# A gated recurrence with a highway layer on one core: wider GpSimd products, e written over d in three pieces, zero matmuls in the ramp, and a new instruction list

## The chip, the cores and the metric

The kernel runs on 1 core of one Trainium2 chip. The metric is the device time of one execution in microseconds (us). Three runs of the kernel before gave 211.63, 212.32 and 211.7 us, a median of 211.7 us. The profile is one further execution, taken by the hardware profiler.

## What is computed

```python
sig = 1 / (1 + exp(-f_logit));  f = lower_bound + (1 - lower_bound) * sig;  i = 1 - f
for t in range(S):                       # x, f_logit: (4, 6336, 256) float32
    h = f[:, t] * h + i[:, t] * x[:, t];  y[:, t] = h
H = maximum(y @ w_h, 0);  T = 1 / (1 + exp(-(y @ w_t + b_t)))    # 25344 tokens, 256 x 256 weights
out = T * H + (1 - T) * y
```

## The kernel before, in words

The 25,344 tokens are cut into 28 units of 2, 2, 4, then 23 times 8, then 4 and 2 blocks of 128 tokens. A unit's data lie once with the tokens and once with the 256 features on the partitions; the features are two halves h = 0, 1 of 128. The work is a hand-ordered list of tokens (the string `order`); a token such as `z16.1:2` names a step, a unit, a half or piece, and, behind the colon, the buffer that its result takes. Every engine gets its instructions in the order of the list. The engines are PE (TensorE), DVE (VectorE), ACT (ScalarE), POOL (GpSimd) and SP, which issues all loads and stores. The steps of a unit are:

- `l`, `x` (line 262): loads of f_logit and x by SP, six buffers each. `w` (L393): a store of up to four blocks by SP, after the copy `c`.
- `u` (L274, ACT): sigmoid(-f_logit), all blocks in one instruction. Three buffers.
- `b` (L282): bv = u * x in pieces of 512 columns (two blocks), on POOL, or on DVE where the token ends in v.
- `i` (L288, PE): transposes of u into PSUM; `f` (L299 ACT, L297 DVE with v): f = 1 - (1 - lower_bound) u from there; `p` (L308, PE): transposes of bv. One-bank PSUM tiles `a`, two of them, hold both.
- `s` (L325, DVE): the scan y over a unit's tokens, one instruction for each half (and one more where a sequence starts). It begins from the last column of the unit before, so the scans of a half hang on each other.
- `z`, `g` (L337 and L140, PE): y @ w_t and y @ (w_h - 1), in two-bank PSUM tiles `b`, three of them, shared with `o`.
- `t` (L350, ACT): sigmoid(z + b_t). `d` (L354, DVE): max(g, -y) in the scaling of y used inside; three buffers.
- e = d * t (L359) in a tile of its own with three buffers: `E` are pieces of 512 columns on POOL up to a column that is set for each unit (the last number in `units`), `e` is the rest in one instruction on DVE. A unit of 8 blocks has 2,048 columns.
- `o` (L378, L379, PE): y and e are transposed back and added in PSUM, four blocks at a time; `c` (L388 ACT, L386 DVE with v) copies this to SBUF.

Once at the start: eight matmuls of zeros (L178), `pc` transposes the parameters, `cc`, `dg`, `WT`, `WH` (L223 to L251, DVE) scale weights and diagonals, `wh`, `wt` load weights (L215, L212), and `k*16` puts sixteen matmuls of zeros on PE. Where a POOL product follows a DVE product in the list, the helper `shared` lets POOL's instruction wait until the DVE one has ended. There is no wait the other way.

Of the kernel before, what the change touches and what calls it, by code (L numbers as in the profile page):

```python
# [19 lines left out]
def kernel(  # L20
# [54 lines left out]
z0.1:1 l4:4 i2.0:1 x4:4 b2.0:2 p1.1:0 b2.1 f2.0:0 z0.0:2 d0.0 s1.1 i2.1:1 t0.1:0 g1.1:0 b3.2v:0 p2.1:0 z1.0:1 t0.0  # L75
f2.1:1 b3.1v s2.1:2 t1.0:1 z1.1:2 p2.0:1 l5:5 t1.1 s2.0 b3.3 g1.0:1 u4:2 d1.1:1 b3.0 l6:0 i3.0:0 p3.1:1 E0.0:0 d1.0
s3.1:3 z2.1:0 z2.0:1 g2.1:2 f3.0:3 b4.2:1 i4.0:0 t2.0:2 g2.0:1 t2.1 d2.0:2 E1.0:1 b4.1 f4.0:1 x5:5 b4.0 l7:1 p3.0:1
x6:0 b4.3 u5:0 i4.1:0 s3.0 o1.0:1 f4.1:0 o0.0:0 d2.1 E2.0:2 p4.0:1 c0.0v:0 c1.0:1 s4.0:1 i5.0:0 g3.1:2 u6:1 d3.1:0
z3.0:1 E2.1 b5.3:2 f5.0:2 t3.0:0 i5.1:1 p4.1:0 g3.0:2 b5.1 o2.0:0 b5.0 z3.1:1 s4.1 f5.1:3 b5.2 d3.0 w0.0 p5.0:1 w1.0
b6.2:0 u7:2 b6.3 i7.1:0 z4.1:2 s5.0:0 t3.1 g4.0:1 l8:2 f7.1:1 p5.1:0 i6.1:1 c2.0:2 x7:1 z4.0:0 x8:2 t4.1:1 d4.0:1  # L80
f6.1:0 b6.1 g4.1:2 s5.1 z5.1:1 b6.0 w2.0 u8:0 t4.0 E3.0:1 l9:3 t5.1:2 e3 b7.3:1 d4.1 p6.1:0 i8.1:1 o3.0:0 o3.1:2
s6.1:2 b7.1 f8.1:2 E4.0:0 c3.0:3 i6.0:1 e4 f6.0:3 b8.1:2 l10:4 g5.0:1 p6.0:0 i7.0:1 c3.1:0 g5.1:0 o4.0:2 d5.0:2 z5.0:1
# [5 lines left out]
b11.1:2 s9.0 l14:2 t8.1 f10.1:0 o6.0:0 d8.1 i11.1:1 c6.0:1 b10.1 e8:0 e7:2 g9.0:1 z9.0:2 p10.0:0 f11.1:1 b11.2 o6.1:0
p10.1:1 t9.0:0 o7.0:2 b11.0 b12.2:0 b11.3 d9.0:0 z9.1:1 u13:2 b12.3 c6.1:2 b12.1 s10.0:2 i11.0:0 g9.1:0 s10.1 w6.0
t9.1 o7.1:1 p11.0:1 l15:3 c7.0:0 f11.0:3 c7.1:3 u14:0 E9.1:1 d9.1 E9.0 x13:1 i12.0:0 z10.0:2 w7.0 g10.0:1 o8.1:0  # L90
s11.0:3 d10.0:1 p11.1:1 t10.0:1 z10.1:1 g10.1:2 s11.1 b12.0 w6.1 c8.1:1 f12.0:0 w7.1 t10.1 g11.0:0 E9.2 o8.0:1 u15:1
E9.3 d10.1 p12.1:0 c8.0:0 x14:2 d11.0:2 w8.1 i13.1:1 s12.1:1 x15:3 b13.3:1 o9.1:2 b13.0 w8.0 z11.0:1 b13.1 f13.1:3
b13.2 c9.1:2 i15.1:1 p12.0:0 g11.1:0 e10:2 f15.1:1 i13.0:1 w9.1 z11.1:2 t11.0:2 s12.0 o9.0:1 p13.0:0 b14.2:2 f13.0:2
# [148 lines left out]
    def do_k(slot):  # L242
        busy(once["idle"])
# [120 lines left out]
    def do_e(n, k, eng, slot):  # L364
        times(n, nc.vector, units[n][6], NH * tokens(n), slot)
# [68 lines left out]
```

## Time and profile before

| what | us |
|---|---|
| median of the three runs | 211.7 |
| span of the profiled execution | 210.1 |
| DVE busy in the span | 193.0 |
| ACT busy in the span | 194.5 |
| PE busy in the span | 192.2 |
| POOL busy in the span | 174.0 |

The profiled execution's own time beside its span isn't given; the median of the runs is 1.6 us above the span. Busy times are unions: an instruction begins before the one ahead of it on its engine has drained, so the durations of a group add up to a little more than its engine's busy time. In a group's row stand the line, the engine, the operation, the shapes, the count, the busy time, the mean duration in ns, and behind the second bar the engine's idle time just before, with what ended it. In a row of the timeline stand the start, the duration, the engine and the instruction.

### The profile page before, as it was taken

The numbers are of one execution on the slowest core, as the hardware profiler recorded it, in microseconds if no ns is written. First come the engines' busy times: TensorE is split into PE (matmuls) and PEld (weight loads), VectorE is DVE, ScalarE is ACT, GpSimd is POOL, SyncE is SP. The second block draws the span as 40 slices with busy tenths as digits, with TensorE's granted clock in tenths as the row PEclk, the third lists the DMA queues.
The fourth block names the chain that finished last, engine by engine and source line by source line (L and its number), as shares of the span: only waits on it lengthen the run. The fifth ranks groups of instructions, "written<-read, shape, count | busy, mean of one in ns | idle before, by whom it ended". The sixth has DMA issues, their size and how long they took to land.

```text
span 210.1 us, 4667 instructions
## 1 busy us (share of the span) xinstructions
PE 192.2 (91%) x1819; PEld 132.4 (63%) x1819; DVE 193.0 (92%) x154; ACT 194.5 (93%) x190; POOL 174.0 (83%) x166
## 2 busy tenths in 40 slices
PE   7967798899989989999999999999999899999981
PEld 2444555576655766767576667657775676776760
DVE  0689999999999999999999999999999999999950
ACT  4678999999999999999999999999999999997882
POOL 3068989789999599978999999889879969999630
PEclk9999999999999999999999999999999999999998
DMA  6999999999999999999999999999999998463486
GB/s 223 392 426 421 410 418 424 420 415 420 410 428 413 420 420 403 331 406 387 387 427 416 409 416 423 418 417 396 333 428 416 416 413 332 188 271 132 172 328 254
DMA packets 15982, 78.69 MB, mean 374 GB/s; under 512 B 1748, under 2 KB 2264, under 8 KB 10072
## 3 DMA queue, kind: packets, MB, share of 16 engines
q1 hardware_dynamic: 15952, 78.39, 92.9%
q8 instruction: 14, 0.23, 0.5%
q14 instruction: 8, 0.07, 0.1%
q10 hardware_dynamic: 8, 0.00, 0.0%
HBM read 52.43 MB, written 25.95 MB: 373 GB/s over the span
## 4 chain that ended last, share of the span: by engine, by line
DVE 34%; PE 34%; DMA 12%; issue 8%; POOL 5%; ACT 3%; SPq 1%; POOLq 0%; DVEq 0%; ACTq 0%
DVE y L325 21%; DMA x<-in_x_dram 12%; DVE d L354 10%; PE op L379 5%; PE op L378 5%; PE g L337 4%; PE z L337 4%; PE bT L308 4%; POOL bv L282 4%; PE g L140 4%; PE uT L288 4%; PE z L140 3%; DVE e L359 3%; ACT t L350 2%; ACT o L388 1%
## 5 line engine op out<-in xcount | busy, mean ns | idle before, releaser
L282 POOL TENSOR_TENSOR bv<-u,x 128x512 bf16<-128x512 f16 x96 | 110.2, 1178 | 22.3 <-DVE w_sb L235 8.9
L325 DVE TENSOR_TENSOR_SCAN y<-f,y,bT 128x1024 bf16<-128x1024 f16 (+5 forms) x54 | 107.2, 1994 | 1.4 <-issue 0.4
L359 POOL TENSOR_TENSOR e<-d,t 128x512 bf16<-128x512 bf16 (+1 forms) x59 | 65.0, 1125 | 8.3 <-DVE e L359 5.0
L354 DVE SCALAR_TENSOR_TENSOR d<-y,ncc,g 128x1024 bf16<-128x1024 bf16 (+2 forms) x56 | 63.1, 1140 | 1.8 <-PE g L337 1.3
L350 ACT ACTIVATE t<-z,bt 128x1024 bf16<-128x1024 f32 (+2 forms) x56 | 58.4, 1066 | 2.7 <-PE z L140 1.5
L299 ACT ACTIVATE f<-uT,ncc 128x1024 f16<-128x1024 f16 (+2 forms) x54 | 57.8, 1079 | 2.0 <-ACT f L299 1.0
L388 ACT COPY o<-op 128x1024 f32<-128x1024 f32 (+1 forms) x50 | 52.3, 1058 | 1.9 <-PE op L379 1.0
L274 ACT ACTIVATE u<-l 128x2048 f16<-128x2048 f32 (+2 forms) x28 | 49.0, 1760 | 4.1 <-DMA l<-in_f_logit_dram 4.1
L378 PE MATMUL op<-diag,y 128*128 128x128 f16 x396 | 49.4, 219 | 0.8 <-ACT t L350 0.5
L379 PE MATMUL op<-ident_b,e 128*128 128x128 bf16 x396 | 49.4, 219 | 0.6 <-POOL e L359 0.6
L379 PEld LDWEIGHTS <-e 128*128 128x128 bf16 x396 | 44.0, 113 | 4.6 <-POOL e L359 1.1
L378 PEld LDWEIGHTS <-y 128*128 128x128 bf16 x396 | 44.2, 113 | 2.5
L337 PE MATMUL z<-y,w_sb 128*128 128x512 bf16 (+1 forms) x112 | 39.2, 367 | 2.0 <-DVE d L354 1.0
L337 PE MATMUL g<-y,w_sb 128*128 128x512 bf16 (+1 forms) x112 | 39.6, 367 | 0.5 <-DVE y L325 0.3
L308 PE MATMUL bT<-ident_f,bv 128*128 128x128 f32 x198 | 31.9, 278 | 4.1 <-DVE y L325 1.9
L288 PE MATMUL uT<-ident_h,u 128*128 128x128 f16 x396 | 31.1, 220 | 4.5 <-DVE y L325 3.3
L288 PEld LDWEIGHTS <-u 128*128 128x128 f16 x396 | 26.3, 98 | 13.9 <-issue 7.4
L140 PE MATMUL g<-y,w_sb 128*128 128x512 bf16 x92 | 34.9, 379 | 0.0
L140 PE MATMUL z<-y,w_sb 128*128 128x512 bf16 x92 | 34.8, 379 | 0.0
L337 PEld LDWEIGHTS <-w_sb 128*128 128x128 f16 x224 | 21.6, 98 | 16.2 <-issue 0.8
L308 PEld LDWEIGHTS bT<-ident_f,bv 128*128 128x128 f32 x198 | 22.3, 141 | 12.0 <-POOL bv L282 4.5
L140 PEld LDWEIGHTS <-w_sb 128*128 128x128 f16 x184 | 17.9, 98 | 18.2 <-issue 3.9
(35 smaller groups left out, 47.1 us busy)
## 6 DMA issues: line engine op xcount, KB each, us to landing
out_dram<-o SPq DMA_DIRECT2D x48, 512.0 KB, 6.1
l<-in_f_logit_dram SPq DMA_DIRECT2D x23, 1024.0 KB, 10.2
x<-in_x_dram SPq DMA_DIRECT2D x23, 1024.0 KB, 11.1
l<-in_f_logit_dram SPq DMA_DIRECT2D x2, 512.0 KB, 9.2
x<-in_x_dram SPq DMA_DIRECT2D x2, 512.0 KB, 6.0
l<-in_f_logit_dram SPq DMA_DIRECT2D x3, 256.0 KB, 6.1
x<-in_x_dram SPq DMA_DIRECT2D x3, 256.0 KB, 5.4
out_dram<-o SPq DMA_DIRECT2D x3, 256.0 KB, 5.4
```

Source lines behind the costliest of these rows:

```text
L140: return pe.add_instruction(mybir.InstMatmult(name=nc.get_next_instruction_name(), start_tensor_calc=start, stop_tensor_calc=stop, tile_si ...
L282: shared(pin(e.tensor_mul(st[n]["bv"][:, k].rearrange("p d j -> p j d"), st[n]["u"][:, q:q + 2], st[n]["x"][:, q:q + 2])), not eng)
L288: pin(nc.tensor.transpose(uT[:, j * P:(j + 1) * P], st[n]["u"][:, j, h * P:(h + 1) * P], ident_h))
L299: pin(nc.scalar.activation(to, of, AF.Identity, scale=ncc[:, h:h + 1], bias=1.0))
L308: pin(nc.tensor.transpose(words[:, k:k + g * (P - 1) + 1:g], pair, ident_f))
L325: pin(nc.vector.tensor_tensor_scan(y[:, c:e], st[n]["f", h][:, c:e], st[n]["bT", h][:, c:e], 0.0 if fresh else carry[h], op0=ALU.mult, op1 ...
L337: pin(nc.tensor.matmul(p[:, a:e], w, half(n, "y", ki)[:, a:e], start=ki == 0, stop=ki == NH - 1))
L350: pin(nc.scalar.activation(half(n, "t", m), st[n]["z", m][:, :tokens(n)], AF.Sigmoid, bias=bt[:, m:m + 1]))
L354: pin(nc.vector.scalar_tensor_tensor(half(n, "d", m), half(n, "y", m), ncc[:, m:m + 1], st[n]["g", m][:, :tokens(n)], op0=ALU.mult, op1=AL ...
L359: shared(pin(eng.tensor_mul(st[n]["e"][:, a:e], st[n]["d"][:, a:e], st[n]["t"][:, a:e])), eng is nc.gpsimd)
L378: pin(nc.tensor.matmul(o, half(n, "y", h)[:, cols], diag[:, h], start=True, stop=False))
L379: pin(nc.tensor.matmul(o, half(n, "e", h)[:, cols], ident_b, start=False, stop=True))
```

## The change

- `b` is cut by a table: one piece of 512 columns for units of 2 blocks, two of 512 for 4 blocks, two of 1,024 for 8 blocks. POOL has 45 pieces of 1,024 and 5 of 512 for 96 of 512; DVE has two of 512 and one of 1,024 for three of 512.
- `E` and the tile e are gone. `e` is d = d * t, in place, in pieces: 256 + 256 columns (2 blocks), 512 + 512 (4 blocks), 1,024 + 512 + 512 (8 blocks). A token with v runs on DVE, one without on POOL. DVE has 11 pieces of 1,024, 12 of 512 and 3 of 256; POOL has 12 of 1,024, 38 of 512 and 3 of 256. `o` reads d. d has four buffers, and u has four.
- `k` takes a PSUM tile of the given buffer in place of a fixed one, and eight `k*4` (four matmuls of zeros each) and one matmul of zeros ahead of z3.1 stand in the list's first part.
- The list is a new one on all engines. DVE has five f for two (0.0, 0.1, 1.1 and 27.0 with 256 columns, 8.0 with 1,024), and the one copy on DVE is c25.1 (1,024 columns) in place of c0.0 (512). l27 is loaded ahead of l13.

```diff
+    parts = [2] * 2 + [4] + [8] * 23 + [4] + [2]
+    for nb in parts:
+        units.append((nb, at, {2: (0, 1), 4: (0, 1, 2), 8: (0, 2, 4)}[nb], {2: (0, 256, 512), 4: (0, 512, 1024), 8: (0, 1024, 1536, 2048)}[nb]))
     order = """
-pc:1 l0:0 u0:0 l3:1 wh cc dg i0.0:1 x0:0 i0.1:0 k*16 u3:1 wt WH b0.0v:0 l1:2 f0.0:0 f0.1:1 p0.1:0 i3.1:1 u1:2 s0.1:0
-WT p0.0:0 x1:1 s0.0 f3.1:2 l2:3 x2:2 i1.1:0 u2:0 g0.1:2 f1.1:3 i1.0:1 d0.1:0 g0.0:0 b1.0:1 x3:3 p1.0:0 f1.0v:1 s1.0:1
...
-e25:2 s27.0 w24.0 o24.1:2 c24.1:0 g26.0:0 o25.0:1 g27.1:2 c25.0:2 d26.0 o25.1:0 e26:1 d27.1:0 g27.0:2 z27.1:1 t27.1:0
-E26.1 w24.1 d27.0 z27.0:2 c25.1:1 w25.0 t27.0 E26.0 o26.0:1 w25.1 c26.0:3 e27:0 E27.0 o27.0:2 c27.0:0 w26.0 w27.0
+l0:0 x0:0 pc:0 wh wt u0:0 l2:1 x1:1 l1:2 l3:3 cc x2:2 x3:3 i0.0:0 b0.0v:0 l4:0 u2:1 u1:2 x4:4 i0.1:1 f0.1v:0 k*16:1
+l5:4 x5:0 WT l6:5 dg WH p0.1:1 f0.0v:1 x6:5 s0.1:0 p0.0:0 k*4:0 s0.0 i1.0:1 i1.1:0 b1.0:0 z0.0:0 f1.1v:0 g0.0:1 d0.0:0
+f1.0:1 p1.1:1 l7:1 t0.0:0 z0.1:2 u3:0 p1.0:0 b2.0:0 s1.1:1 k*4:0 g0.1:0 i2.1:1 t0.1 s1.0 i3.0:0 d0.1 z1.1:0 f2.1:0
+e0.0 f3.0:1 b2.1v z1.0:1 g1.0:2 i2.0:1 d1.0:1 f2.0:2 e0.1v i3.1:0 t1.0:0 p2.0:1 b3.0v:1 s2.0:2 g1.1:2 d1.1 o0.0:1 t1.1
+k*4:0 f3.1:3 p2.1:0 s2.1 k*4:0 u4:1 b3.1 c0.0:0 p3.0:1 z2.1:0 w0.0 l9:0 e1.1 e1.0v o1.0:2 t2.1:0 i4.0:0 s3.0:0 b4.1:0
...
+o3.0:1 g5.1:2 t4.0 x10:4 f7.1:1 c3.0:0 w3.0 s6.1:3 i7.0:0 b7.1 z5.1:0 f7.0:2 k*4:1 d5.1:2 t5.1:1 p6.0:0 e4.1v u8:0
...
+u27:2 c7.0:0 f10.0:2 c6.0:1 u13:3 b11.0:2 g9.1:1 d9.0:0 p10.0:0 s10.0 w7.0 i11.0:1 b11.1 f11.0:0 z9.1:0 t9.1:0 e8.2
+e8.0 z9.0:2 t9.0 i12.0:1 d9.1 f12.0:2 p11.1:0 z10.0:0 t10.0:1 e9.0 g10.0:1 l15:0 u15:0 o8.1:2 p11.0:1 s11.1:3 c8.1:0
...
+w24.1 e25.2 s27.0:2 o25.0:2 w24.0 g26.1:0 e26.0 c25.0:0 o23.0:1 c23.0:3 s27.1 w25.0 g27.0:2 d26.1 o25.1:0 d27.0:1
+z27.0:2 e26.1 o26.0:1 c25.1v:1 t27.0:0 w23.0 z27.1:2 e27.0 w25.1 g27.1:0 t27.1 c26.0:2 d27.1 e27.1v o27.0:0 c27.0:0
+w26.0 w27.0
 """
     def do_k(slot):
-        busy(once["idle"])
+        two_banks(slot, "idle")
     def do_b(n, k, eng, slot):
-        q = 2 * k
+        a, c = units[n][2][k:k + 2]
         e = nc.vector if eng else nc.gpsimd
-        shared(pin(e.tensor_mul(st[n]["bv"][:, k].rearrange("p d j -> p j d"), st[n]["u"][:, q:q + 2],
-                                st[n]["x"][:, q:q + 2])), not eng)
+        shared(pin(e.tensor_mul(st[n]["bv"][:, a:c].rearrange("p k d j -> p k j d"),
+                                st[n]["u"][:, 2 * a:2 * c].rearrange("p (k j) d -> p k j d", j=2),
+                                st[n]["x"][:, 2 * a:2 * c].rearrange("p (k j) d -> p k j d", j=2))), not eng)
-    def times(n, eng, a, e, slot):
-        flat(n, "e", "e", slot)
-        shared(pin(eng.tensor_mul(st[n]["e"][:, a:e], st[n]["d"][:, a:e], st[n]["t"][:, a:e])), eng is nc.gpsimd)
-
-    def do_E(n, k, eng, slot):
-        times(n, nc.gpsimd, k * 512, min(units[n][6], k * 512 + 512), slot)
-
     def do_e(n, k, eng, slot):
-        times(n, nc.vector, units[n][6], NH * tokens(n), slot)
+        a, c = units[n][3][k:k + 2]
+        e = nc.vector if eng else nc.gpsimd
+        shared(pin(e.tensor_mul(st[n]["d"][:, a:c], st[n]["d"][:, a:c], st[n]["t"][:, a:c])), not eng)
     def do_o(n, q, eng, slot):
-                pin(nc.tensor.matmul(o, half(n, "e", h)[:, cols], ident_b, start=False, stop=True))
+                pin(nc.tensor.matmul(o, half(n, "d", h)[:, cols], ident_b, start=False, stop=True))
```

More of the change, by code (lines that the diff above doesn't have):

```diff
@@ L78 @@
[L78 to L82, printed above, removed]
@@ L88 @@
[L88 to L92, printed above, removed]
@@ new lines @@
+z22.0:2 w20.0 z23.0:1 b25.0 t22.0 o21.1:0 p24.1:0 t23.0:1 c21.1:0 g23.1:2 i25.0:1 e22.2 s24.1 o21.0:1 f25.0:0 g23.0:0
+d23.1:1 i25.1:0 d23.0 c21.0:1 p25.0:1 z23.1:1 s25.0:1 g24.1:2 u26:1 f25.1:1 t23.1 z24.1:0 e22.0 i26.1:0 d24.1:2 e22.1
+w20.1 o22.1:1 x27:0 t24.1:2 c22.1:2 p25.1:1 o22.0:0 x26:1 b26.1:1 f26.1:0 c22.0:3 g24.0:2 i26.0:0 z24.0:1 s25.1 w21.1
+b26.0 p26.0:1 e23.2 w21.0 f26.0:2 d24.0 z25.0:0 p26.1:0 e23.0 z25.1:2 t24.0 s26.0:3 s26.1 g25.1:1 t25.0:0 b27.0:0
+t25.1 o23.1:0 d25.1:0 z26.1:2 e24.2 i27.0:0 c23.1:0 i27.1:1 e23.1v e24.0v f27.0v:0 g25.0:1 z26.0:0 t26.1:1 o24.1:2
@@ L124 @@
+w22.1 p27.0:0 f27.1:1 e24.1 p27.1:1 d25.0 t26.0 g26.0:0 o24.0:1 c24.1:1 c24.0:2 e25.1v w22.0 w23.1 e25.0v d26.0:3
+w24.1 e25.2 s27.0:2 o25.0:2 w24.0 g26.1:0 e26.0 c25.0:0 o23.0:1 c23.0:3 s27.1 w25.0 g27.0:2 d26.1 o25.1:0 d27.0:1
+z27.0:2 e26.1 o26.0:1 c25.1v:1 t27.0:0 w23.0 z27.1:2 e27.0 w25.1 g27.1:0 t27.1 c26.0:2 d27.1 e27.1v o27.0:0 c27.0:0
+w26.0 w27.0
 """
```

121 lines of the change are left out of this document (45 added, 76 removed).

## The prediction

> **What bounds the kernel now.** I read the page's busy times first, then the busy times by stage, then what VectorE (DVE) waited for.
>
> ```profile
> span 210.1 us, 4667 instructions
> PE 192.2 (91%) x1819; PEld 132.4 (63%) x1819; DVE 193.0 (92%) x154; ACT 194.5 (93%) x190; POOL 174.0 (83%) x166
> ```
> ```profile
> 0.00:40.00 40.00, 31.96 (x228) 18.72 (x229) 31.36 (x41) 32.55 (x35) 26.52 (x33) 1.00 0.97 391
> 40.00:100.00 60.00, 57.84 (x576) 40.82 (x575) 59.83 (x41) 59.87 (x57) 53.41 (x48) 1.00 1.01 405
> 100.00:160.00 60.00, 58.64 (x578) 41.56 (x576) 59.92 (x42) 59.86 (x55) 55.82 (x51) 1.00 1.01 407
> 160.00:200.00 40.00, 39.10 (x379) 27.43 (x377) 39.50 (x29) 37.00 (x40) 35.84 (x33) 1.00 0.71 285
> 200.00:210.10 10.10, 4.69 (x65) 3.90 (x63) 2.43 (x6) 5.20 (x7) 2.45 (x3) 0.91 0.74 288
> ```
> ```profile
> DVE ncc L223 <- PE prmT L219: 3.9, 1, 3.9
> DVE y L325 <- PE bT L308: 1.3, 2, 1.0
> DVE d L354 <- PE g L337: 1.3, 3, 0.6
> DVE w_sb L249 <- DMA w_raw<-in_moe_w_h_dram: 1.0, 1, 1.0
> DVE zeros L175 <- PEq L418: 0.9, 1, 0.9
> ```
>
> The columns of the stages are PE, weight loads, DVE, ScalarE (ACT), GpSimd (POOL), granted clock, DMA share, GB/s. From 40 to 200 us DVE is idle for 0.17+0.08+0.50 = 0.75 us of 160, and the scans of one half hang on each other, so nothing there can come earlier: **time is DVE's work plus its idle time in the ramp (8.64 us in the first 40) and in the tail (7.67 in the last 10).** ACT is as full from 40 to 160, DMA's share is 1.01 there, and the clock is 1.00 up to 200 us. POOL has slack. The three runs' median of 211.7 lies 1.6 us above the span, which I take as constant.
>
> **The change part by part.**
>
> ```profile
> L359 DVE TENSOR_TENSOR e<-d,t 128x1536 bf16<-128x1536 bf16 x6 | 5.7, 954 | 0.0
> L359 DVE TENSOR_TENSOR e<-d,t 128x2048 bf16<-128x2048 bf16 x4 | 4.8, 1215 | 0.1
> L359 DVE TENSOR_TENSOR e<-d,t 128x1792 bf16<-128x1792 bf16 x1 | 1.1, 1068 | 0.0
> L359 DVE TENSOR_TENSOR e<-d,t 128x256 bf16<-128x256 bf16 x3 | 0.8, 280 | 0.3 <-ACT t L350 0.3
> L359 DVE TENSOR_TENSOR e<-d,t 128x1024 bf16<-128x1024 bf16 x1 | 0.7, 684 | 0.0
> L359 DVE TENSOR_TENSOR e<-d,t 128x768 bf16<-128x768 bf16 x1 | 0.6, 630 | 0.0
> L297 DVE TENSOR_SCALAR f<-uT,ncc 128x256 f16<-128x256 f16 x1 | 0.5, 479 | 0.0
> L386 DVE COPY o<-op 128x512 f32<-128x512 f32 x1 | 0.7, 684 | 0.0
> L282 DVE TENSOR_TENSOR bv<-u,x 128x512 bf16<-128x512 f16 x3 | 2.1, 721 | 0.0
> L299 ACT ACTIVATE f<-uT,ncc 128x256 f16<-128x256 f16 x5 | 2.3, 473 | 0.3 <-PE uT L288 0.3
> L388 ACT COPY o<-op 128x1024 f32<-128x1024 f32 x48 | 51.1, 1077 | 1.6 <-PE op L379 0.7 <-ACT o L388 0.3 <-ACT t L350 0.2
> L388 ACT COPY o<-op 128x512 f32<-128x512 f32 x2 | 1.2, 594 | 0.3 <-PE op L379 0.3
> ```
>
> *DVE's work.* Of the old sixteen e these rows give 13.7 us. The new list puts 11 pieces of 1,024, 12 of 512 and 3 of 256 on DVE. A 512 piece has no row; it lies between 280 and 684 ns, and a line through these two gives 415. That makes 7.5+5.0+0.8 = 13.3 us. DVE starts an operation about 0.08 us before the last one's end (a scan of the timeline below starts at 41.80, takes 2.34, and its successor starts at 44.05), so ten more instructions hide 0.8 more: e costs 1.2 us less. Four f of 256 columns stand on DVE for one: 3 x 0.40 = +1.2. Three bv of 512 become two and one of 1,024, which lies between 0.72 and 2 x 0.72; near the upper end, 1.3: +0.6. The copy is now c25.1 with 1,024 columns for c0.0 with 512: between 0.68 and 1.37, taken 1.2, so +0.5. Sum **+1.1 us**, of which that copy lies behind the last scan in place of smaller work there; up to the last scan I count **+0.5** (0 to +1.0). ACT loses 3 x 0.473 + 1.077 - 0.594 = 1.9 us; it isn't alone on the path, so I credit nothing.
>
> *POOL.*
>
> ```profile
> L282 POOL TENSOR_TENSOR bv<-u,x 128x512 bf16<-128x512 f16 x96 | 110.2, 1178 | 22.3 <-DVE w_sb L235 8.9 <-DVE e L359 7.8 <-DVE bv L282 1.8
> L359 POOL TENSOR_TENSOR e<-d,t 128x512 bf16<-128x512 bf16 x54 | 61.8, 1167 | 3.8 <-DVE e L359 1.9 <-ACT o L388 1.8
> L359 POOL TENSOR_TENSOR e<-d,t 128x256 bf16<-128x256 bf16 x5 | 3.4, 670 | 4.5 <-DVE e L359 3.1 <-ACT t L350 1.5
> ```
>
> From 670 to 1,167 ns for 256 more columns is 1.94 ns a column, so 1,024 columns take 1,167+994 = 2,161 ns; the bounds are 1,178 and 2 x 1,178 = 2,356. I take 2.16. Old: 110.2+61.8+3.4 = 175.4 us. New: bv 45 x 2.16 + 5 x 1.178 = 103.1, e 12 x 2.16 + 38 x 1.167 + 3 x 0.670 = 72.3, sum 175.4: **POOL's work does not change**. What wide instructions save, the 3,584 columns of e moved from DVE to POOL use up. At 2.356 it would be +11 us.
>
> In place of its own tile, e overwrites d; d has four buffers for three, held until the output matmuls. I cost this at nothing, since POOL's e and PE are a unit ahead of the fourth reuse; uncovered it would show as a wait of d for op.
>
> *The ramp.*
>
> ```profile
> 5.74 3.95 PE L140 MATMUL idle<-zeros 128*128 128x512 bf16 x15
> ...
> 11.80 0.38 PE L337 MATMUL g<-y,w_sb 128*128 128x256 bf16 x2
> ```
> ```profile
> 5.01 0.16 DVE L223 TENSOR_SCALAR ncc<-prmT 128x2 f32<-128x2 f32 x1 [3.88 <-PE prmT L219]
> ...
> 9.84 0.69 DVE L325 TENSOR_TENSOR_SCAN y<-f,bT 128x256 bf16<-128x256 f16 x1 [1.01 <-PE bT L308]
> ...
> 41.80 2.34 DVE L325 TENSOR_TENSOR_SCAN y<-f,y,bT 128x1024 bf16<-128x1024 f16 x1
> 44.05 1.01 DVE L359 TENSOR_TENSOR e<-d,t 128x1536 bf16<-128x1536 bf16 x1
> ```
> ```profile
> 6.37 1.91 ACT L274 ACTIVATE u<-l 128x2048 f16<-128x2048 f32 x1 [2.27 <-DMA l<-in_f_logit_dram]
> ```
>
> x0, wh and wt are now issued ahead of the 1 MB l3, so the wait of 1.0 for wh goes: DVE runs bv 0, f0.1, the weights and f0.0 from 5.3 to about 9.2. But p0.1 still stands behind sixteen zero matmuls on PE, which end at 5.74+3.95 = 9.7, and so the first scan is again at 9.84: 0.6 idle. From there I walk the new list with the old durations. A zero matmul takes 3.95/15 = 0.26 us, a k*4 about 1.0. The k*4 behind p0.0 ends at 10.7; i1.1 waits for the scan s0.0 (to 11.1) to free its bank, so f1.1 starts at 11.4 (0.3 idle, to 11.85); z0.0 and g0.0 follow on PE, 0.25 to 0.35 us each, and d0.0 starts at 12.05 (0.2 idle). The two scans of unit 1 end at 13.75; the second k*4 and g0.1 are done by 13.6, so d0.1 doesn't wait. u3 runs on ACT from 12.1 to 14.0, i3.0 behind it on PE to 14.5, then z1.1, z1.0, g1.0 to 15.25: d1.0 starts at 15.3, bv 2.1 having ended at 14.9 (0.4 idle). From there on f, p and g are ready when DVE comes, but for 0.1 before s3.0, and unit 5's scans begin at 33.6. The other six k*4 fall where PE waits for POOL or a bank (p2.1 for f3.1, p3.0 for b3.1). With the old 0.9+3.9 this is 4.8+0.6+0.3+0.2+0.4+0.1 = 6.4 us of idle time in place of 8.64. I take **-1.9**, since such a walk misses small waits (-2.8 to +0.1: there two more k*4 cost DVE their full 1.0). The zero matmuls buy no clock, which is 1.00 already.
>
> *The tail.*
>
> ```profile
> 199.60 0.74 DVE L325 TENSOR_TENSOR_SCAN y<-f,y,bT 128x256 bf16<-128x256 f16 x1
> ```
> ```profile
> 205.94 0.59 ACT L388 COPY o<-op 128x512 f32<-128x512 f32 x1 [0.31 <-PE op L379]
> ```
>
> Old: the last copy starts 205.94-200.34 = 5.6 us after the last scan's end. New, counted from that end: g27.0 waits for o23.0 on PE and ends at 0.65; d27.0 1.2, behind d26.1; o25.1 1.55; c25.1 on DVE 1.65 to 2.85, beside o26.0; z27.1 3.1; g27.1, held by c25.1's bank, 3.4; d27.1 3.95; e27.1, now on DVE, 4.15; o27.0 4.65; the last copy at 4.75. **-0.8** (-1.1 to +0.3).
>
> *Loads and stores* are the same 56 and 51 with the same bytes, in another order on SP's queue. A store waits there for its copy and holds the loads behind it. l27 comes early and takes slot 0 until u27, so l15 can't be issued before u27 and w7.0.
>
> **Sum:** +0.5-1.9-0.8 = -2.2 with the middle as tight as before: span 207.9, time **209.5 us**.
>
> **The rivals.**
>
> *1. Slower: GpSimd's wide pieces meet DVE's e.*
>
> ```profile
> 43.09 1.16 POOL L359 TENSOR_TENSOR e<-d,t 128x512 bf16<-128x512 bf16 x1
> ```
>
> This POOL piece ends at 44.25, DVE's e of 1,536 columns was issued at 44.05 and took 1.01 where the group's mean is 0.954: DVE seems to wait for POOL's instruction in flight. Under this list POOL waits for each DVE e that stands ahead of it, but nothing makes DVE wait in the list's order, so a late POOL is met by DVE's e. The new list has 26 e pieces on DVE in some 14 places for 16, and what is in flight is up to 2.16 us long for 1.18. It decides if 1,024 columns take over about 2.25 us: at 2.356 POOL comes 0.19 late per wide piece, some four pieces to a place, 0.8 us; over half of the 14 places +5, from 209.5 to 214.5; at 2.25, 0.36 us a place and +2.5, **212.0**. For it: POOL was 93% busy from 100 to 160. Against: the two POOL rows give a fixed part of 173 ns that a wide piece pays once. Chance 0.17.
>
> [...]
>
> *2. No difference: the ramp's gain is eaten.* Two more k*4 on DVE's path are 2.0 us: 211.5. For it: eight blocks of 1.0 on a PE that was idle for 8.0 us in 40. Against: by the walk six of them fall into waits. Chance 0.13.
>
> *3. Slower: the new order stalls the full middle.*
>
> ```profile
> l<-in_f_logit_dram SPq DMA_DIRECT2D x23, 1024.0 KB, 10.2
> L299 ACT ACTIVATE f<-uT,ncc 128x1024 f16<-128x1024 f16 x45 | 52.8, 1181 | 0.8 <-PE uT L288 0.6
> ```
>
> Between u27/c7.0 and u15 the list has eight ACT operations, about 8.7 us less overlaps, and l15 needs a median 10.2 us to land: u15 may hold ACT for 1.5 us, and all behind it. Two such places give +3: 212.5. Against: the 10.2 holds for loads queued behind others. Chance 0.15.
>
> **How the numbers follow.** Forecast 0.55, rivals 0.17, 0.13, 0.15. About 0.3% (0.63 us) is what a measurement can tell from no change: faster 0.55 (the forecast), same 0.13 (rival 2), slower 0.32 (1 and 3). The range goes from 208.3 (ramp and tail at their good ends) to 213.2, leaving out rival 1 near 2.356 us a piece. The forecast alone: 208.3 to 210.8.
>
> **What would show it.** POOL's bv of 1,024 columns at 2.16 us and POOL's busy time near 174; DVE's first scan at 9.8, its idle time of the first 40 us near 6.7; DVE idle below 1 us from 40 to 200 (a wait of e or of d there speaks for 1, ACT waiting for l for 3); from the last scan's end to the last copy 4.8 us. Wrong if DVE's e lasts clearly over 0.68 us at 1,024 columns, or if DVE's busy time is not 194 to 195.

## The result, and the profile after

The changed kernel takes **210.89 us** (median of 17 runs; one of them took 513.54 and is left out of the ratio, the others lie between 209.94 and 211.97) and the kernel before, on the same chip, 211.71 (17 runs, 211.59 to 212.37). The ratio is 0.9956, with a 95% interval of 0.9944 to 0.9969: faster by 0.8 us, where 2.2 were forecast (209.5). Two things stand beside the median. Runs of the kernel before agree within some tenths; those of the changed kernel spread over 2 us. And the profiled execution of the changed kernel took 211.79 us, one of its longer runs. So I read two profiles: that one, and one of the control (the same kernel run again for the experiments, 210.39 us).

The page of the changed kernel, its busy times, and then its stages, in the columns used before:

```profile
span 209.6 us, 4674 instructions
PE 194.3 (93%) x1852; PEld 135.3 (65%) x1852; DVE 194.5 (93%) x167; ACT 192.8 (92%) x187; POOL 173.1 (83%) x114
```
```profile
0.00:40.00 40.00, 33.93 (x249) 20.31 (x250) 32.77 (x45) 31.40 (x34) 24.39 (x25) 1.00 0.97 388
40.00:100.00 60.00, 58.09 (x567) 40.94 (x566) 59.01 (x45) 59.88 (x55) 53.72 (x31) 1.00 1.02 404
100.00:160.00 60.00, 57.67 (x579) 41.51 (x578) 59.44 (x46) 59.23 (x56) 54.60 (x33) 1.00 1.02 416
160.00:200.00 40.00, 39.67 (x400) 28.45 (x398) 39.58 (x31) 37.72 (x39) 37.43 (x26) 1.00 0.71 269
```

The same stages of the control:

```profile
0.00:40.00 40.00, 34.92 (x250) 20.44 (x251) 33.30 (x45) 31.80 (x34) 24.20 (x25) 1.00 0.97 386
40.00:100.00 60.00, 57.98 (x570) 41.01 (x569) 59.14 (x45) 59.81 (x56) 54.30 (x32) 1.00 1.01 405
100.00:160.00 60.00, 58.35 (x590) 42.15 (x588) 60.00 (x45) 59.89 (x56) 55.56 (x32) 1.00 1.02 417
160.00:200.00 40.00, 39.91 (x403) 28.77 (x402) 39.74 (x31) 37.64 (x40) 37.21 (x27) 1.00 0.72 278
```

DVE's idle time of the first 40 us is 7.23 and 6.70 us, for 8.64 before: here the change does what was forecast, wholly in the one run and in part in the other. Between the two the wait for the weight w_t differs most, 1.16 and 0.23 us. From 40 to 200 us DVE's idle time is 0.99+0.56+0.42 = 1.97 and 0.86+0+0.26 = 1.12, for 0.75 before; 0.17 of the control's 0.26 lies behind its last scan, so that up to this scan it has 0.95. Where most of it is lost in the changed kernel's profile, by its timeline (start, duration; in brackets the idle time before it and what ended that), POOL's row first and then DVE's:

```profile
86.32 6.37 POOL L257 TENSOR_TENSOR bv<-u,x 128x1024 bf16<-128x1024 f16 x3 [1.99 <-DMA x<-in_x_dram]
...
96.49 2.35 DVE L301 TENSOR_TENSOR_SCAN y<-f,y,bT 128x1024 bf16<-128x1024 f16 x1 [0.99 <-ACT t L326]
```

POOL waits 2 us for x15. The pieces of unit 13 stand behind those of unit 15 in its queue, and ten microseconds later the scan of unit 13 is late. (The scan is put down to ACT's t; ACT had been busy without a gap, and what came last was the chain through POOL.) The control, a short run, has the same wait and loses nearly as much by it:

```profile
85.93 6.38 POOL L257 TENSOR_TENSOR bv<-u,x 128x1024 bf16<-128x1024 f16 x3 [1.85 <-DMA x<-in_x_dram]
...
96.11 2.35 DVE L301 TENSOR_TENSOR_SCAN y<-f,y,bT 128x1024 bf16<-128x1024 f16 x1 [0.86 <-ACT t L326]
```

So x15 doesn't tell a long run from a short one. What the long one has beside it is another load that is late, an l for which ACT waits, and some microseconds later a d that waits on DVE (its g on PE was held by ACT's copy behind that u); the control has neither row:

```profile
151.92 1.92 ACT L249 ACTIVATE u<-l 128x2048 f16<-128x2048 f32 x1 [0.66 <-DMA l<-in_f_logit_dram]
...
155.91 1.28 DVE L330 SCALAR_TENSOR_TENSOR d<-y,ncc,g 128x1024 bf16<-128x1024 bf16 x1 [0.56 <-issue]
```

In both profiles the loads take longer than before, when l had a median of 10.2 us from issue to landing (the rows are the changed kernel's; the control has 13.9 and 14.5):

```profile
l<-in_f_logit_dram SPq DMA_DIRECT2D x23, 1024.0 KB, 14.7
x<-in_x_dram SPq DMA_DIRECT2D x23, 1024.0 KB, 14.5
```

The groups that carried the sum of the work:

```profile
L257 POOL TENSOR_TENSOR bv<-u,x 128x1024 bf16<-128x1024 f16 x45 | 96.1, 2156 | 7.3 <-DMA x<-in_x_dram 2.7 <-ACT f L275 2.5 <-DVE bv L257 1.7
L336 POOL TENSOR_TENSOR d<-d,t 128x1024 bf16<-128x1024 bf16 x12 | 25.6, 2136 | 0.1
L336 DVE TENSOR_TENSOR d<-d,t 128x1024 bf16<-128x1024 bf16 x11 | 7.7, 698 | 0.0
L336 DVE TENSOR_TENSOR d<-d,t 128x512 bf16<-128x512 bf16 x12 | 5.1, 437 | 0.2 <-ACT t L326 0.2
L257 DVE TENSOR_TENSOR bv<-u,x 128x512 bf16<-128x512 f16 x2 | 1.9, 950 | 0.0
```

The tail in the control, first the last scan and the last copy by the timeline, then PE's share by stretches of the tail:

```profile
197.79 1.38 DVE L301 TENSOR_TENSOR_SCAN y<-f,y,bT 128x256 bf16<-128x256 f16 x2
...
201.15 1.23 DVE L357 COPY o<-op 128x1024 f32<-128x1024 f32 x1 [0.40 <-PE op L350]
...
204.31 0.59 ACT L359 COPY o<-op 128x512 f32<-128x512 f32 x1 [0.51 <-PE op L350]
```
```profile
199.17:200.00 0.83, 0.83 (x16) 0.82 (x14) 0.66 (x2) 0.59 (x2) 0.60 (x2) 1.00 0.65 257
200.00:201.00 1.00, 1.00 (x19) 0.99 (x18) 0.48 (x1) 0.99 (x1) 1.00 (x1) 1.00 1.04 414
201.00:202.00 1.00, 1.00 (x19) 1.00 (x17) 0.85 (x1) 0.47 (x1) 0.15 (x2) 1.00 1.00 393
```

The scans end at 199.17 and the last copy starts 5.14 later, for 5.6 before and 4.8 forecast. PE has no gap in the first 2.8 us of this.

### The profile page after: what moved, and what is told of

It is laid out like the page before. It is cut to its first block, busy times and chain, and to the rows that moved or that the text cites. A ratio compares the mean times of both kernels' runs of the same rounds, so it can differ in the third digit from the quotient of the medians.

```text
span 209.6 us, 4674 instructions
## 1 busy us (share of the span) xinstructions
PE 194.3 (93%) x1852; PEld 135.3 (65%) x1852; DVE 194.5 (93%) x167; ACT 192.8 (92%) x187; POOL 173.1 (83%) x114
## 5 line engine op out<-in xcount | busy, mean ns | idle before, releaser
L257 POOL TENSOR_TENSOR bv<-u,x 128x1024 bf16<-128x1024 f16 (+1 forms) x50 | 101.9, 2059 | 17.4 <-ACT u L249 8.0
L336 POOL TENSOR_TENSOR d<-d,t 128x512 bf16<-128x512 bf16 (+2 forms) x53 | 71.4, 1364 | 12.9 <-DVE d L336 10.2
L275 ACT ACTIVATE f<-uT,ncc 128x1024 f16<-128x1024 f16 (+2 forms) x51 | 55.5, 1097 | 1.0 <-PE uT L264 1.0
L359 ACT COPY o<-op 128x1024 f32<-128x1024 f32 (+1 forms) x50 | 50.7, 1025 | 2.2 <-PE op L350 2.2
L350 PE MATMUL op<-ident_b,d 128*128 128x128 bf16 x396 | 49.4, 219 | 0.1
L350 PEld LDWEIGHTS <-d 128*128 128x128 bf16 x396 | 44.1, 113 | 3.3 <-POOL d L336 0.7
L284 PEld LDWEIGHTS bT<-ident_f,bv 128*128 128x128 f32 x198 | 22.9, 141 | 12.4 <-POOL bv L257 2.5
## 6 DMA issues: line engine op xcount, KB each, us to landing
x<-in_x_dram SPq DMA_DIRECT2D x23, 1024.0 KB, 14.5
```

What stands on the lines that cost most here:

```text
L257: shared(pin(e.tensor_mul(st[n]["bv"][:, a:c].rearrange("p k d j -> p k j d"), st[n]["u"][:, 2 * a:2 * c].rearrange("p (k j) d -> p k j d" ...
L275: pin(nc.scalar.activation(to, of, AF.Identity, scale=ncc[:, h:h + 1], bias=1.0))
L284: pin(nc.tensor.transpose(words[:, k:k + g * (P - 1) + 1:g], pair, ident_f))
L336: shared(pin(e.tensor_mul(st[n]["d"][:, a:c], st[n]["d"][:, a:c], st[n]["t"][:, a:c])), not eng)
L350: pin(nc.tensor.matmul(o, half(n, "d", h)[:, cols], ident_b, start=False, stop=True))
```

## The experiments

All are edits of the changed kernel, except e5, e15 and e16, which are edits of the kernel before. The kernel before gave 211.66 to 211.76 us in the five sets of runs. The ratio is to it.

**a0 and a2: the control, twice.**

> The changed kernel once more, as the yardstick of this set. Its runs spread from 209.9 to 212.0 us, where those of the kernel before lie within 0.2 us but for a few. Theory: the spread comes from loads that land late in some executions, so here again a median of 210.9 with a spread of about 2 us, and in the profile GpSimd waiting 1 to 2 us for an x near 84 us. Rival: the 2 us come from chance in GpSimd and VectorE meeting; then the profile shows longer e on VectorE in other places and no wait for x.

> The changed kernel unaltered, as the control for the three beside it on the same chip. From its 17 and 5 runs so far: median 210.4 to 210.9, single runs from 209.8 to 212.

210.39 us (0.9932 [0.9920, 0.9944]) and 210.79 (0.9949 [0.9937, 0.9961]). With the 17 runs above, the changed kernel is at 210.4 to 210.9. The controls' five runs each spread over 0.8 us. The theory of a0 is half borne out: the wait for x15 is there, but in a run of 210.39 us, so that it is no cause of the spread.

**e3: bv in 512 columns again, the rest as changed.**

```diff
+        for a in range(a, c):
+            shared(pin(e.tensor_mul(st[n]["bv"][:, a].rearrange("p d j -> p j d"), st[n]["u"][:, 2 * a:2 * a + 2],
+                                    st[n]["x"][:, 2 * a:2 * a + 2])), not eng)
```

> Each bv piece of 1,024 columns is made by two instructions of 512 columns that stand at its place, nothing else is changed. GpSimd's work grows by 45 x (2 x 1.178 - 2.156) = 9 us, VectorE's by about 0.1. Theory: GpSimd has some 18 us of idle time from 10 us on but most of it lies where VectorE's e runs, so it comes late to these places, VectorE waits for it, and the kernel is 2 to 5 us slower than the control. Rival: the slack takes it up, and the time stays within 0.5 us.

214.55 us (1.0139 [1.0122, 1.0155]), 4.2 above the control. Its groups of e on DVE:

```profile
L336 DVE TENSOR_TENSOR d<-d,t 128x1024 bf16<-128x1024 bf16 x11 | 8.7, 791 | 0.0
L336 DVE TENSOR_TENSOR d<-d,t 128x512 bf16<-128x512 bf16 x12 | 8.5, 718 | 0.1
```

POOL has 6 us more work (179.3 us busy, for 173.0 in the control), and that alone isn't on the path. But being late, it is met by DVE's e, whose duration rises by 11 x 0.093 + 12 x 0.281 = 4.4 us: as much as the loss between the medians, and most of the 5.0 us between the two profiles' spans (213.2 and 208.2). I read this as rival 1's mechanism, with its price, in a kernel where POOL has no room: the rows show the longer e (0.791 us for 0.698 and 0.718 for 0.437), not which POOL piece each of them met. So the wide bv doesn't make the changed kernel fast by itself; it pays for the e that the new list gives to POOL.

**e5: the wide bv alone, in the kernel before.** The 512-column pieces are joined in pairs, each at the place of the first and third.

```diff
-b4.2:1 ... b4.1 ... b4.0 ... b4.3
+B4.2:1 ... B4.0
+        shared(pin(nc.gpsimd.tensor_mul(st[n]["bv"][:, k:k + 2].rearrange("p k d j -> p k j d"),
```

> The kernel before with one part of the change alone: GpSimd's bv pieces of 512 columns are put together in pairs of 1,024, each at the place of the first and of the third piece in the list of before; e, the list's order and the matmuls are those of before. GpSimd goes from 166 instructions to about 120, with 1,024 columns at 2.16 us for two of 1.18 us, so its busy time falls by about 9 us from 174.0. My theory: GpSimd is not on the path in the kernel before, so the span stays within 0.4 us of 209.9 and DVE's busy time at 193.0; pieces that come later by a pair may cost waits of some tenths. Beside it two views of the 0.35 us that lie outside the span since the change: if they go with the number of GpSimd's instructions, the run's time stands 2.1 to 2.2 above its span here and not 1.8; if they belong to the order or to PE, it stays at 1.75 to 1.85. The rival: the wide pieces alone, without the new order, hold f, p and scans up, and the time rises by 1 us or more.

212.56 us (1.0035 [1.0023, 1.0047]): 0.8 slower than the kernel before beside it (211.76), near the rival's side. The largest new wait, by its timeline:

```profile
50.25 2.35 DVE L330 TENSOR_TENSOR_SCAN y<-f,y,bT 128x1024 bf16<-128x1024 f16 x1 [0.66 <-PE bT L313]
```

A piece that is twice as long delivers its first half later; that is how I read it, and no run tells it from other causes. Neither part is good without the other: the width alone costs 0.8 us, the list without the width 2.9 us against the kernel before.

**e1: x15 earlier.** The load that was late is moved ahead on SP's queue, to right behind b12.0.

```diff
-... c7.1:3 b12.0 g8.0:2 ...
+... c7.1:3 b12.0 x15:0 g8.0:2 ...
-... i13.0:0 x15:0 o9.0:2 ...
+... i13.0:0 o9.0:2 ...
```

> The load x15 is issued right after bv 12 is formed, ahead of the stores w7.1, w6.1 and w7.0, in place of behind w7.0 and l15; nothing else moves. Theory: b15 no longer waits for x15 (1.99 us at 84 us), b13 behind it on GpSimd is in time, the scan of unit 13 loses its 0.99 us of waiting, and the median falls by 0.6 to 1.0 us against the control. Rival: the DMA engines are full there (share 1.02), so that some other load is late by the 2.5 us that x15 takes, and the time stays within 0.3 us of the control.

213.46 us (1.0077 [1.0064, 1.0090]). My theory fell, and the rival's mechanism came at a far higher price than its 0.3 us. By ACT's and DVE's timelines, from a run of 215.19 us, the longest of the six, it is l15 that is late now:

```profile
86.88 1.91 ACT L249 ACTIVATE u<-l 128x2048 f16<-128x2048 f32 x1 [3.27 <-DMA l<-in_f_logit_dram]
...
93.00 2.35 DVE L301 TENSOR_TENSOR_SCAN y<-f,y,bT 128x1024 bf16<-128x1024 f16 x1 [3.73 <-PE bT L284]
```

With the transfers full in the control (share 1.01 to 1.02), I read this as a load that goes ahead and pushes another back.

**e4: unit 27 late.** l27 and u27, which hold slot 0 until 73 us, go to the end of the list.

```diff
-... f8.0v:1 l27:0 z7.0:1      -u27:2 c7.0:0
+... l26:1 l27:2 s24.0:2       +... u26:1 u27:2 f25.1:1
```

> The changed kernel with the load and the sigmoid of unit 27 issued late: l27 right after l26 and u27 right after u26 (slots of their own), instead of l27 before z7.1 and u27 before c7.0. The early pair held slot 0 of the l tiles until u27 ended at 72.5 to 73.7 us, and l15 came behind it. My theory is that this pair makes the loads of units 13 and 15 late, so that without it GpSimd's wait for x15 (1.85 to 1.99 us at 86 us) shrinks or l15 stops being the load that is late, VectorE's idle time from 80 to 100 us falls from 0.86 (the control's profile) to under 0.4, and the time falls by 0.3 to 0.7 us from the control's 210.4 to about 209.8. The rival is that the transfers are full there whatever is loaded (DMA share 1.02): another load is late, the time stays within 0.3 of the control or rises, as it rose when x15 alone was moved ahead. If the late unit 27 is itself missed at the end, the last scan ends later than 199.2 by what u27 waits.

210.26 us (0.9939 [0.9922, 0.9956]), and one of six runs still took 211.47. That is within what the control does by itself, and decides nothing.

**e10 and e16: half of the stores.** Only two of each four rows of units 0 to 21 are stored, in the changed kernel and in the kernel before.

```diff
+        w = 2 if n < 22 else j1 - j0
+        pin(nc.sync.dma_start(rows(out, n, j0, j1)[:, :w], st[n]["o", q][:, :w]))
```

> The changed kernel storing only half of the output rows of units 0 to 21 (two of each group's four; everything is still computed), so that about 10 MB of 78.7 MB of transfers fall away. My theory: the waits of the middle (x15, l15, 0.9 to 2.0 us on VectorE between 40 and 200 us) and the spread of 2 us between runs are loads that come late because the transfers are full (DMA share 1.02). Then with this the idle time of VectorE from 40 to 160 us falls under 0.3, the runs agree within 0.6 us, and the time is the control's fastest or better: 208.5 to 209.7. The rival: the waits are made by the order itself (buffers that come free late, ACT's place in the list); then they stay within 0.3 us and so does the median.

> The kernel before storing only half of the output rows of units 0 to 21 (everything is still computed), as was done with the changed kernel. My theory: the kernel before has no waits for late loads in its middle (0.75 us of idle time on VectorE from 40 to 200 us), so it gains little, 0 to 0.4 us (211.3 to 211.7), against the 0.9 us of the changed kernel. The rival: fewer stores shorten any of these kernels by as much, and the time is 210.6 to 211.0.

The changed kernel: 209.87 us (0.9914 [0.9902, 0.9927]), 0.9 below the control beside it (210.79), and its four runs lie between 209.73 and 210.05. The kernel before: 211.69 (1.0001 [0.9992, 1.0011]). The stages of the changed kernel with half of the stores:

```profile
40.00:100.00 60.00, 58.24 (x571) 41.54 (x580) 59.88 (x45) 60.00 (x56) 54.64 (x32) 1.00 0.92 358
100.00:160.00 60.00, 58.05 (x573) 41.62 (x581) 59.76 (x45) 60.00 (x57) 55.34 (x33) 1.00 0.90 338
```

With the transfers at a share of 0.90 to 0.92, POOL waits 1.11 us ahead of unit 15's pieces, for 1.99 and 1.85, and not for x15 any more; DVE's idle time from 40 to 160 us is 0.12+0.24 = 0.36 us, for 1.55 in the changed kernel's profile and 0.86 and 0.59 in those of the controls a0 and a2. (I had put the idle time under 0.3 and the time under 209.7; both came out just above.) The kernel before gains nothing from the same relief. So the waits of the middle belong to the new list on full transfers: its loads arrive without slack. The spread fits this, 0.3 us in four runs for 0.8 in the controls' five and 2 in the 17, but four runs are few, and that the spread has the same cause isn't shown.

**e2, e8, e11 and e13: the zero matmuls.** e2 leaves out the eight `k*4` and the `*1` of z3.1, 33 matmuls in all. e8 does the same and gives c25.1 and c26.0 buffers of their own. e11 makes the 33 matmuls 2 columns wide. e13 leaves them out and puts 33 matmuls of 2 columns at the start.

```diff
e2, e8, e13:  -p0.0:0 k*4:0 s0.0 ...                 +p0.0:0 s0.0 ...
e8:           -c25.1v:1 ... c26.0:2                  +c25.1v:x3 ... c26.0:l3
e11:          -matmul(t[:, :512], zeros[:, :P], zeros)
              +matmul(t[:, :w], zeros[:, :P], zeros[:, :w])      # w = 2; 512 for k*16
e13:          -for _ in range(8):                    +for k in range(8 + 33):
              +    w = 512 if k < 4 else 2
```

> Without the eight blocks of four zero matmuls and the single one ahead of z3.1 (the sixteen ahead of the first scan stay). Theory, from the walk: only the first two blocks touch VectorE's path, 0.36 and 0.23 us there, so 0.3 to 0.6 us faster than the control, with the granted clock at 1.00 as before. Rival A: the blocks keep the clock up; without them the clock of the first 40 us falls and the kernel is slower. Rival B: they cost 1.0 us each wherever PE is the bound, and the kernel is 2 us faster.

> The changed kernel without its eight k*4 and without the zero matmul of z3.1, and with buffers of their own for c25.1 and c26.0, which without zero matmuls waited 1.77 and 0.75 us for older stores at the end of that profile. One theory: those waits were the whole loss of that run (212.16), so that without them the kernel is as fast as the control or 0.3 us faster (209.9 to 210.6), and the zero matmuls are worth nothing. The other: the zero matmuls do buy something over most runs that the one profile did not show (a clock that falls, loads that meet otherwise), and the time stays at 211.5 to 212.2; the granted clock and VectorE's idle time before 200 us would then show where.

> The changed kernel with the matmuls of its eight k*4 and of z3.1*1 made 2 columns wide for 512: as many instructions at the same places, almost no work of PE. My theory (what counts is where PE's instruction packets fall, not the zero work): the packet before the tail stays near 196 to 197 us, the stores after 198 us land in 2.7 to 3.2 us as in the control, and the time is the control's 210.4 to 210.9 or up to 0.5 less, since PE is freer in the ramp. The rival (the zero work itself is worth something, by the clock or by its delay of PE): the time is 211.5 to 212.2 as without the blocks.

> The changed kernel without the eight k*4 and the zero matmul of z3.1, but with 33 matmuls of 2 columns more at the very start, where four of the eight first ones are made 2 columns wide as well so that the start stays as long. PE's instruction count is the control's. By my theory the packet of q8 that fell at 198 us without the blocks goes back to about 196, the stores at the end land in 2.7 to 3.2 us, and the 212.15 of the kernel without the blocks becomes 210.2 to 210.9. The rival (the work or the place of the zero matmuls matters): it stays at 211.5 to 212.2.

e2: 212.16 us (1.0028 [1.0007, 1.0050]); e8: 212.15 (1.0020 [0.9999, 1.0042]); e11: 210.80 (0.9963 [0.9943, 0.9982]); e13: 210.91 (0.9954 [0.9935, 0.9974]). Without the 33 matmuls e2 loses 1.8 us to the control beside it (210.39) and e8 1.4 to its own (210.79; its runs go from 210.89 to 215.13, and without the three longest it is 1.2). With 33 that do almost nothing, there or at the start, the time is the control's, measured on other chips (e11 and e13 had none beside them). So it is their number that counts.

The loss lies behind the last scan. From the end of the last scan to the end of the span, all fourteen profiles of the changed kernel and its edits that have the 33 matmuls show 8.9 to 9.1 us (the control a2 208.2-199.18), e2 10.8 (209.8-199.02) and e8 10.4 (210.1-199.70). What moves with the number is a packet of the queue q8, whose kind the profile gives as instruction (14 packets and 0.23 MB in the changed kernel's profile, 16 KB each); since it moves with PE's matmuls, I take q8 for the queue of PE's instructions. The packet nearest to the end (packets, MB, its share of 16 engines), in the control a2 in the four microseconds from 196 on, and in e2 in the four from 198 on:

```profile
q8 instruction: 1, 0.02, 1.6%
```
```profile
q8 instruction: 1, 0.02, 3.1%
```

In the control it starts between 196 and 197 us, ahead of the store issued at 197.3, and takes one of the 16 engines for 0.016 x 16 x 4 = 1.0 us. In e2 it starts between 198 and 199, beside the stores issued at 197.1 and 198.7, and takes 2.0 us (in e8 1.5, beside those of 197.8 and 199.4; in e13 it starts between 196 and 197 again, and takes 1.0). What matters is its place against the tail: in e11's profile it starts at 198 too, but there the last scan ends at 200.70. In the controls, e11 and e13 it starts 1.7 to 2.7 us ahead of the last scan's end, in e2 and e8 0.5 to 1.2. The stores from 188 us on, least, median and greatest time from issue to landing, in the control a2 and in e2:

```profile
DMA to landing us min/median/max: 2.4/2.7/3.2
```
```profile
DMA to landing us min/median/max: 2.5/3.8/5.0
```

e8 has 2.6/3.9/4.6 there, e11 2.4/2.7/3.2 and e13 2.4/2.8/3.1. The greatest time rises by 1.8 and 1.4 us, about what the packet takes (2.0 and 1.5). In e2, c25.1 starts after 1.77 us of idle time and c26.0 after 0.75 of waiting for a store; I read the first as a wait for the buffer that such a store holds, for with a buffer of its own (e8) it starts after 0.34. In e8 the last copy then waits for a store, by ACT's timeline:

```profile
204.97 0.59 ACT L362 COPY o<-op 128x512 f32<-128x512 f32 x1 [0.64 <-DMA out_dram<-o]
```

PE itself doesn't wait for the packet in the changed kernel's profile, where its only wait from 199 to 209 us is one of 0.6 for a d of DVE. What lands later in e2 and e8 are the stores, the last thing to end, by about the packet's transfer (1.8 and 1.4 us for 2.0 and 1.5). That the packet is what holds them is read from where it lies in these profiles; no run moves it and leaves the matmuls alone.

The clock stayed at 1.00 over the first 40 us in e2, e8 and e13, but not in e11: there it was 0.87 from 9 to 12 us and 0.56 from 12 to 15, in a run of 211.93 us, the longest of its eleven.

**e15: the same 33 at the start of the kernel before,** whose packet moves at 200 us, beside its last stores.

```diff
-    for _ in range(8):
+    for k in range(8 + 33):
+        w = 512 if k < 4 else 2
```

> The kernel before with 33 matmuls of 2 columns more at the very start, and four of its eight first zero matmuls made 2 columns wide so that the start stays as long; nothing else differs. By my theory the q8 packet at 200.x us moves to about 197 to 198, the stores at the end land sooner (2.4 to 3.2 us in place of 2.7 to 4.2), and the time falls by 0.2 to 0.4 us to 211.3 to 211.5: so much of the change's gain would be a matter of the count of instructions. The rival: the stores ahead of the last one matter to nobody, and the time stays at 211.6 to 211.8.

212.25 us (1.0024 [1.0012, 1.0036]): slower, and not faster by 0.2 to 0.4. The packet did move, to 197, and the stores did land sooner (2.6/2.7/3.0 for 2.6/3.0/4.2). But the last store took 2.7 us in both, and from the last copy's start to the end of the span it was 4.2 us in both, so that nothing was gained: in this kernel the packet beside the stores costs no time. And the shorter start was not neutral. Its PE timeline shows the sixteen zero matmuls ahead of p0.1:

```profile
5.00 0.64 PE L151 MATMUL idle<-zeros 128*128 128x512 bf16 x1
5.43 1.06 PE L140 MATMUL idle<-zeros 128*128 128x512 bf16 x2
6.71 3.76 PE L140 MATMUL idle<-zeros 128*128 128x512 bf16 x12 [0.22 <-issue]
```

They end at 10.5 us for 9.7 before, though they start 0.3 earlier, and the first scan starts at 10.62 for 9.84. e13 has the same start and a first scan at 10.28, so its 210.91 carries such a handicap too.

**e7: c25.1 and c26.0 in buffers of their own, zero matmuls kept.**

```diff
-c25.1v:1 ... c26.0:2
+c25.1v:x3 ... c26.0:l3
```

> The changed kernel with two more buffers for its output copies at the end: c25.1 writes into an x tile and c26.0 into an l tile that are free by then, so that neither can wait for an older store from the same o buffer; four o buffers remain for the others. In the control's profile no copy of the tail waited for a store, so there the tail stays at 5.14 us from the last scan's end to the last copy's. My theory of the spread of 2 us between runs of the changed kernel is that it arises in the middle, at the loads, so the spread stays and the median is within 0.3 us of the control's 210.4. The rival is that the spread arises from stores in the tail, as in the one profile without zero matmuls, where c25.1 waited 1.77 us and c26.0 0.75 us: then the slow runs go, the largest of the times falls to about 210.5 and the median by 0.3 to 0.6.

210.87 us (0.9959 [0.9947, 0.9971]), 210.45 to 211.29 in five runs: as the control, and spread as the control's five. Waits for these two buffers don't make the spread. Beside e8, which differs by the zero matmuls alone, it also shows the way from the last scan to the end at 9.0 us for 10.4.

**e6, e9, e12 and e14: 45 memsets of one column on POOL at the start,** alone (e6), with unit 27 late (e9), with narrow zero matmuls (e12), and with both (e14).

```diff
+    small = sb([P, 1], FP32, "small")
+    for _ in range(45):
+        nc.gpsimd.memset(small, 0.0)
     nc.vector.memset(zeros, 0.0)
```

> The changed kernel with 45 memsets of one column on GpSimd added right behind the identity matrices, at 2 us, where GpSimd is idle until 10.5 us; nothing else differs, and the 45 make up for the instructions that the wide bv pieces saved (114 to 159). They last under 5 us in all by the four memsets of one column at the start (0.10 us each, 0.03 us apart), so no wait in the span should change. One view: the 0.35 us outside the span go with the count of GpSimd's instructions, and the run's time stands 1.75 to 1.85 above its span, as in the run with 512-column pieces, and the time is 210.0. The other: they do not, and it stands 2.1 to 2.2 above the span, with the time at the control's 210.4.

> The changed kernel with unit 27's load and sigmoid late, and with the 45 memsets of one column on GpSimd at the start: both parts that came out a little faster on their own. If both hold and add up (0.1 to 0.6 and 0.3 to 0.4 us), the median is 209.6 to 210.0 and the time outside the span 1.8; if the gains of 0.1 to 0.6 were spread between runs, only the 0.35 outside the span is left, and the median is 210.2 to 210.5.

> The narrow zero matmuls together with 45 memsets of one column on GpSimd at the start. If narrow blocks are no worse than the control and the 0.35 us outside the span come back (1.8 above the span for 2.18), the median is 209.8 to 210.3; if the spread from late loads covers it, it is 210.3 to 210.8.

> The same as the run before it, with unit 27's load and sigmoid late as well. From the run with late l27 and 45 memsets (210.08, single runs from 209.4) less what narrow blocks free in the ramp: 209.5 to 210.1; if narrow blocks free nothing, 210.1 again.

e6: 210.09 us (0.9922 [0.9894, 0.9950]); e9: 210.08 (0.9935 [0.9911, 0.9958]); e12: 210.57 (0.9932 [0.9910, 0.9955]); e14: 210.39 (0.9929 [0.9905, 0.9952]). What is certain is the time outside the span. The queue q14 in the changed kernel and in e6, which differ by the 45 instructions on POOL alone, so that I take it for the queue of POOL's instructions:

```profile
q14 instruction: 6, 0.05, 0.1%
```
```profile
q14 instruction: 7, 0.06, 0.1%
```

Every run has a span and a time. In all kernels with six packets (the changed one, a2, e1, e2, e4, e7, e8, e10, e11, e13) a run's time stands 2.1 to 2.2 us above its span; in those with seven or eight (the kernel before, e3, e5, e6, e9, e12, e14, e15, e16) 1.73 to 1.93. The 45 memsets alone turn the one into the other, and e5 has the shorter time with seven packets though only 120 instructions show on POOL, for 114 in the changed kernel. So the time goes with the packets; that they cause it isn't shown. What the chip does in those 0.35 us no profile shows, since it lies outside the span. Beyond that, e12 and e14 came out at or above the forecast for no gain: the narrow matmuls free nothing. In the profiles of e11, e12 and e14 DVE is idle for 7.6 to 8.2 us in the first 40, for 6.7 to 7.5 in those of the other edits with the full ones but e1 (7.85); why isn't shown. e6 and e9 are the fastest versions with all of the work, some 0.3 to 0.8 us below the control's medians, and their intervals overlap its own.

## Why the prediction was right in sign and wrong in size

The control's profiled run, term by term, against the forecast's steps (us):

| step | forecast | control | changed kernel's profile |
|---|---|---|---|
| ramp, DVE idle to 40 us | -1.9 | -1.94 | -1.41 |
| middle, DVE idle from 40 us to the last scan | 0 | +0.20 | +1.22 |
| DVE's work up to the last scan | +0.5 | +0.57 | +0.42 |
| last scan's end | -1.4 | -1.17 | +0.23 |
| last scan's end to last copy | -0.8 | -0.46 | -0.46 |
| last copy to end of span | 0 | -0.27 | -0.27 |
| outside the span | 0 | +0.59 | +0.59 |
| time (211.7 and these) | 209.5 | 210.39 | 211.79 |

(The work is what remains of the last scan's end, 200.34 before, 199.17 and 200.57, after the idle times.)

- **Right:** POOL's piece of 1,024 columns at 2.16 us (2.156) and its unchanged work (173.1 busy for 174.0); the work of DVE up to the last scan; the ramp in a good run, with the first scan at 9.1 to 9.6. In the long run the ramp gave only 1.41: of the wait for the weights, which I had let vanish, 1.16 us was left, now for w_t. The work of the zero matmuls hardly costs time: e11 and e13, without it, are level with the control. "The zero matmuls buy no clock" holds by the granted clock in e2, e8, e12, e13 and e14 (1.00 in the first 40 us), and not in e11 (0.96). That e overwrites d shows no wait of d for op.
- **"The middle as tight as before" failed.** DVE waits 0.2 us more in the good profile and 1.2 more in the long one, where it is the step that costs most; nothing in the forecast's list of durations could show it. e10 and e16 show the cause: late loads under full transfers. I had seen the place in rival 3 (l15 issued late, behind l27), but u15 didn't wait; the load behind it, x15, did. As a price for the median, rival 3's +3 was too much.
- **"1.6 us above the span, which I take as constant" failed** by 0.59, the largest miss of the good profile. Some 0.2 of it is that the profile of before, at 210.1, was longer than its usual run (the median of its spans is 209.9), so that the true figure was 1.8; the rest is the step from 1.8 to 2.15, which e6 ties to POOL's instructions, a term that the forecast didn't have.
- **"The tail -0.8" was mis-sized**: -0.46. I let o25.1 end 1.55 us after the last scan; c25.1, which follows it, started at 1.98, since PE was full from the scan's end on. I had counted the waits of the chain and not PE's load. The way from the last copy to the end gave 0.27 back: the last store landed in 2.4 us for 2.7.
- **Together:** the median of 210.89 lies 1.4 us above the forecast. The time outside the span, the tail and the end are the same in both profiles and make 0.59+0.34-0.27 = 0.66 of it. The other 0.7 is, as an estimate, what ramp and middle cost in a run of middling length: they cost 0.2 in the good profile (-0.04+0.20) and 1.7 in the long one (0.49+1.22).
- **Rival 1** didn't come in the changed kernel (DVE's e of 1,024 columns took 0.698 us for 0.684 before), but e3 shows how near it was. No run shows the 2.25 us a piece from which its 212.0 was reckoned; POOL's pieces took 2.156. One of DVE's two bv pieces of 512 columns did meet POOL: it ran from 14.07 us on beside a POOL piece that ended at 14.67, and took 1.18 us where the other took 0.72 (mean 0.95). **Rival 2** fell: the ramp's gain is there, and the extra blocks don't eat it.

Open: which pairing of loads and stores makes one run of the changed kernel longer than another, since most runs have no profile; what the 0.35 us outside the span are; and whether the late l of the long run belongs to most long runs.

## What to carry over

A list that is planned from durations is only as good as its loads: where transfers are full before the change and after it, ask of each load how long before its use it lands, and allow for a spread where the slack is gone (here 2 us in 17 runs, and 0.3 in four with half of the stores). Test a gain by instructions that do nothing (zero matmuls, warm-up) with as many that do even less: here their number was the effect, and what moved with it in the profiles was an instruction packet beside the last stores. And take the time outside the span from several runs before using it as a constant.

## What the runs showed of the hardware that I had not expected

- With a 16 KB packet of the queue q8 beside the last stores, these landed in up to 5.0 us for 3.2, and the way from the last scan to the end took 10.8 and 10.4 us for 9.0; the medians rose to 212.16 and 212.15, for 210.39 and 210.79. In the kernel before, the same neighbourhood cost nothing (e15).
- The time outside the span is 2.1 to 2.2 us with six packets of the queue q14 and 1.73 to 1.93 with seven or eight.
- Where four of the first eight zero matmuls were made narrow, the next fifteen full ones took from 5.43 to 6.71+3.76 = 10.47, or 5.0 us (one record is missing), for 3.95 (e15), though the granted clock of its profile was 1.00 in the first 40 us. The first of them start 0.43 us apart (5.00 and 5.43), where those of the changed kernel's first k*4 start 0.21 apart (9.92 and 10.13): PE ran at half that pace there, and the granted clock's row doesn't show it. So the 1.00 of that row alone doesn't prove that zero matmuls buy no pace.
